# First microseconds of an mLSTM and two gated feed-forward layers: Exp table, forget factors, Sigmoids and first weights reordered

## The chip, the cores and the metric

One core of a Trainium2 chip runs the whole kernel in one launch. The metric is the device time of a run in microseconds; the time before is the median of three runs. The profile is of one execution on the chip.

## The reference, cut to what matters

```python
# q, k, v, o_gate: (B=4, H=8, S=768, D=40); i_gate, f_gate: (4, 8, 768)
for t in range(S):
    m_new = maximum(f_gate[t] + m, i_gate[t])
    f_stab = exp(f_gate[t] + m - m_new)
    i_stab = exp(i_gate[t] - m_new)
    m = m_new
    C = f_stab * C + i_stab * outer(v[t], k[t])
    n = f_stab * n + i_stab * k[t]
    y[t] = sigmoid(o_gate[t]) * (C @ q[t]) / maximum(abs(n @ q[t]), 1)
x = y as (3072 tokens, 320)
x = (sigmoid(x @ w_gate) * (x @ w_val)) @ w_out          # d_ff 1536
h = x @ w_in                                             # d_ff 2048
out = (h * clip(h + 3, 0, 6) / 6) @ w2_out
```

## The kernel before

The sequence is cut into 6 chunks of 128 steps. Within a chunk the recurrence is written as products of matrices: scores k by q, multiplied by a decay matrix, times v scaled by the input factor; between chunks a state is carried. All arithmetic is fp32; the dense layers split each operand into two parts and multiply three times.

**The start.** Lines 264 to 265 load the gates, 32 rows (batch and head) by 768 steps. `stabilise` (L207 to L219) runs a running maximum over some of the steps on VectorE and then two Exps on ScalarE, which give the forget factors `fz` and the input factors `i`. It is called for the first 128 steps first, and for the other 640 after batches 0 and 1 of chunk 0 are traced (L564). The forget factors of chunk 0 are stored to DRAM (L552), and `dec_load` (L192) reads them back per batch, broadcast to all 128 partitions, into the tile `dec`, 512 KB each. In `att0` a scan on VectorE (L320, two per batch) turns these rows into the decay matrix with the identity `ident4` as its second operand; L333 multiplies the scores (L303) by it. `transpose_rows` (L225) brings the input factors into columns (`iT`). The Sigmoid of the output gates (L338) is issued on ScalarE behind the first `stabilise`'s last Exp (`first_exp`); Exp and Sigmoid lie in different tables of ScalarE.

**After that**, `att1` (L340 on) forms numerator and denominator, and `att2` (L423 on) transposes the result into the token-column tiles `xh` and `xl` (L432, L433) that the first layer reads. Batches 0 and 1 of chunk 0 come first, then `later_chunks` (transposes of the other chunks' factors, the scan L239, the end values L252 and their copy L259), then the steps of the first layer: `m1_h` (matmuls L444 to L451) and `m1_out` (L486, L496). For chunk 0 the first four steps are done for batches 0 and 1, then for batches 2 and 3 (`halves`, L569), whose attention is traced among the steps.

**The weights** come as 64-bit words. `fetch` (L85) loads one tile of 640 KB into one of three buffers, `to_f32` unpacks it (L105 on ScalarE, L108, L112 and L116 on VectorE), and `split_in` or `split_out1` splits it (L134 to L154). The first three are fetched with batch 1's load (L558, L559).

**The order of the work.** Each engine runs its own queue in order. The order in a queue is written by a scheduler that follows the order of the program among what it expects to be ready, so it need not be the program's. All loads but the input gates' go through SP's queue (L189, L190, L193, L552, L88); the input gates' load is issued from ScalarE's queue. PSUM has eight banks: three `mm`, three `acc`, two `att`. In the start `any_ps` hands them out in turn, by a count; the later attention pieces take `att` banks.

Of the kernel before, what the change touches and what calls it, by code (L numbers as in the profile page):

```python
# [8 lines left out]
F32 = mybir.dt.float32  # L9
# [4 lines left out]
AF = mybir.ActivationFunctionType  # L14
# [4 lines left out]
B, H, S, D = 4, 8, 768, 40  # L19
L = 128  # L20
NC = S // L
BH = B * H
NP = H // 2
D1 = D + 1
P = 128
# [7 lines left out]
def mlstm_then_two_gated_ffn(  # L33
# [11 lines left out]
    nc = tc.nc  # L45

    const = ctx.enter_context(tc.tile_pool(name="const", bufs=1))
# [8 lines left out]
    def ps_mm():  # L56
        return mm_ps.tile([P, 512], F32, tag="mm", name="mm")

    def ps_acc():
        return acc_ps.tile([P, 512], F32, tag="acc", name="acc")  # L60

    def ps_att():
        return att_ps.tile([P, 512], F32, tag="att", name="att")
# [3 lines left out]
    def any_ps():  # L67
        k = banks_used[0] % 8
        banks_used[0] += 1
        return ps_mm() if k < 3 else ps_acc() if k < 6 else ps_att()  # L70

    ident4 = const.tile([P, 4, P], F32, name="ident4")
    ident = ident4[:, 0, :]
    half = const.tile([P, 1], F32, name="half")
    iT = const.tile([P, NC, B, H, 1], F32, name="iT")
    gT = const.tile([P, NC, B, H, 1], F32, name="gT")
    gend = const.tile([P, NC, B, NP, 1], F32, name="gend")
# [7 lines left out]
    def fetch(src):  # L85
        r = gpool.tile([P, 640], I64, tag="raw", name="raw", bufs=3)
        if src.shape == r.shape and src.dtype == I64:
            nc.sync.dma_start(out=r, in_=src)  # L88
            return r
        x = r.bitcast(F32)[:, 0:640]  # L90
        nc.sync.dma_start(out=x, in_=src)
        return x
# [76 lines left out]
    at = {}  # L169
# [5 lines left out]
    def slot_f32(n, p=P):  # L175

        return wpool.tile([P, 1280], F32, tag="w", name="early", bufs=18)[:p, :n]

    def att_load(c, b):
        if c == 0 and b > 1:  # L180
            t = slot_f32(2 * NP * L).rearrange("p (a n l) -> p a n l", a=2, l=L)
            v = slot_f32(3 * DM).rearrange("p (a n) -> p a n", a=3)
            d = slot_f32(H * L).rearrange("p (h l) -> p h l", l=L)
        else:
            t = ap.tile([P, 2, NP, L], F32, tag="qk", name="qk")
            v = ap.tile([P, 3, DM], F32, tag="vko", name="vko")
            d = ap.tile([P, H, L], F32, tag="dec", name="dec")
        at[c, b] = {"qk": t, "vko": v, "dec": d}
        nc.sync.dma_start(out=t, in_=qkT[c, b])  # L189
        nc.sync.dma_start(out=v, in_=vko[c, b])  # L190

    def dec_load(c, b):  # L192
        nc.sync.dma_start(  # L193
            out=at[c, b]["dec"].rearrange("p h l -> p (h l)"),
            in_=fz_dram[c, b * H : (b + 1) * H, :]
            .rearrange("h l -> (h l)")
            .rearrange("(o n) -> o n", o=1)
            .to_broadcast([P, H * L]),
        )

    f_sb, i_sb, m_sb, fz_sb, fs_sb, g_sb = [slot_f32(S + 1, BH) for _ in range(6)]
    fz = fz_sb[:, :S].rearrange("p (c l) -> p c l", l=L)
# [4 lines left out]
    def stabilise(a, b):  # L207

        m_old, m_new = m_sb[:, a:b], m_sb[:, a + 1 : b + 1]
        f, i = f_sb[:, a:b], i_sb[:, a:b]  # L210
        nc.vector.tensor_tensor_scan(
            out=m_new, data0=f, data1=i,
            initial=-1e30 if a == 0 else m_sb[:, a : a + 1], op0=ALU.add, op1=ALU.max,
        )
        nc.vector.tensor_tensor(out=f, in0=f, in1=m_old, op=ALU.add)
        nc.vector.tensor_tensor(out=f, in0=f, in1=m_new, op=ALU.subtract)
        nc.scalar.activation(out=fz_sb[:, a:b], in_=f, func=AF.Exp)
        nc.vector.tensor_tensor(out=i, in0=i, in1=m_new, op=ALU.subtract)
        return nc.scalar.activation(out=i, in_=i, func=AF.Exp).ins  # L219

    def transpose_rows(src, dst, chunks):

        ps = any_ps()
        for k, c in enumerate(chunks):
            nc.tensor.transpose(  # L225
                out=ps[:, k * BH : (k + 1) * BH], in_=src[:, c, :], identity=ident[:BH, :BH]
            )
        n = len(chunks)
        nc.scalar.copy(
            out=dst[:, chunks[0] : chunks[0] + n].rearrange("p c b h o -> p (c b h o)"),  # L230
            in_=ps[:, : n * BH],
        )

    def later_chunks():
# [26 lines left out]
            in_=ps[:, BH // 2 : NC * BH // 2],  # L261
        )

    nc.sync.dma_start(out=f_sb[:, :S], in_=gates[:, 0])
    nc.scalar.dma_start(out=i_sb[:, :S], in_=gates[:, 1])
    make_identity(nc, ident)
# [1 line left out]
    nc.vector.tensor_copy(out=ident4[:, 1:, :], in_=ident4[:, 0:1, :].to_broadcast([P, 3, P]))  # L268
    nc.gpsimd.memset(fs_sb[:, :S], 0.0)
    nc.gpsimd.memset(cst, 0.0)  # L270
    nc.vector.memset(half, 0.5)

    sel = const.tile([BH, BH // 2], F32, name="sel")
    nc.vector.tensor_reduce(
        out=sel, in_=ident[:BH, :BH].rearrange("p (n two) -> p n two", two=2),
# [4 lines left out]
        out=odd[:, :, 0], in_=ident[:BH, :BH].rearrange("p (n two) -> p two n", two=2),  # L280
# [4 lines left out]
        out=par.rearrange("p (two n) -> p two n", two=2), in_=odd.to_broadcast([BH, 2, 64])  # L285
    )

    def scale_heads(out, in_, by, apart):

        if apart:  # L290
            for h in range(H):
                nc.scalar.mul(out=out[:, h, :], in_=in_[:, h, :], mul=by[:, h, :])
        else:
            nc.vector.tensor_tensor(out=out, in0=in_, in1=by.to_broadcast(list(out.shape)), op=ALU.mult)


    def att0(c, b, ps):
        a = at[c, b]
        qk, dec = a["qk"], a["dec"]
        s_ps = [ps(), ps()]  # L300
        for h in range(H):
            p0 = 64 * (h % 2)
            nc.tensor.matmul(  # L303
                out=s_ps[h % 2][:, (h // 2) * L : (h // 2 + 1) * L],
                lhsT=qk[p0 : p0 + D, 1, h // 2, :],
                rhs=qk[p0 : p0 + D, 0, h // 2, :],
                start=h < 2,
                stop=h >= H - 2,
                skip_group_check=True,
            )  # L310
        vko_t = a["vko"]
        vi = ap.tile([P, H, D1], F32, tag="vi", name="vi")
        v_h = vko_t[:, 0, :].rearrange("p (h d) -> p h d", d=D)
        if c == 1:
            scale_heads(vi[:, :, 0:D], v_h, iT[:, c, b], True)
        nc.scalar.copy(out=vi[:, :, D:D1], in_=iT[:, c, b])

        for n in range(2):
            x = dec[:, 4 * n : 4 * n + 4, :].rearrange("p h l -> p (h l)")
            nc.vector.tensor_tensor_scan(  # L320
                out=x, data0=x, data1=ident4.rearrange("p h l -> p (h l)"),
                initial=0.0, op0=ALU.mult, op1=ALU.add,
            )
        if c != 1:
            scale_heads(vi[:, :, 0:D], v_h, iT[:, c, b], False)
        a["vi"] = vi
        if c < NC - 1:
            vd = ap.tile([P, H, D1], F32, tag="vd", name="vd")
            scale_heads(vd, vi, dec[:, :, L - 1 : L], c == 0 and b > 0)
            a["vd"] = vd  # L330
        for n in range(2):
            x = dec.rearrange("p (n two) l -> p two n l", two=2)[:, n]
            nc.vector.tensor_tensor(  # L333
                out=x, in0=s_ps[n].rearrange("p (n l) -> p n l", l=L), in1=x, op=ALU.mult
            )

        with tc.issue_after(first_exp):
            nc.scalar.activation(out=vko_t[:, 2, :], in_=vko_t[:, 2, :], func=AF.Sigmoid)  # L338

    def att1(c, b, ps):  # L340
# [182 lines left out]
    jobs = []  # L523
# [22 lines left out]
    fetched = []  # L546


    x_tiles((1, 0))
    att_load(0, 0)  # L550
    first_exp = stabilise(0, L)
    nc.sync.dma_start(out=fz_dram[0], in_=fz[:, 0, :])  # L552
    dec_load(0, 0)
    transpose_rows(i_c, iT, range(0, 1))
    for b in range(1, B):
        att_load(0, b)
        dec_load(0, b)
        if b == 1:  # L558
            fetched += [fetch(jobs[-1 - n][0]) for n in range(3)]  # L559
    for b in range(2):  # L560
        work(1 + b, n_w1)
        for att in (att0, att1, att2):
            att(0, b, any_ps)
    stabilise(L, S)  # L564
    later_chunks()


# [21 lines left out]
    for i, (c, f, ts) in enumerate(steps):  # L589
        if i == halves[0] - 1:  # L590
            for b in range(2):
                att_load(1, b)
                dec_load(1, b)
        for _ in range(quota[i]):
            if pieces:
                cp, b, piece = pieces.pop(0)
                if cp > 0 and b == 0 and piece == 0:
                    x_tiles((1, cp))
                (att0, att1, att2)[piece](cp, b, ps_att)
                nxt = divmod(cp * B + b + 2, B)  # L600
                if cp > 0 and piece == 2 and nxt[0] < NC:
                    att_load(*nxt)
                    dec_load(*nxt)
# [143 lines left out]
```

## Time and profile before

| | us |
|---|---|
| median of three runs | 881.5 |
| lowest and highest | 878.61, 883.31 |
| the profiled execution | 880.11 |
| its span | 878.3 |

The profiled execution's time is 1.8 us more than its span, which is what the profile shows from the first to the last instruction. PE is TensorE's matmuls, PEld its weight loads, DVE VectorE, ACT ScalarE, SP the engine whose queue issues most DMAs; SPq and ACTq are the queues themselves. The granted clock of TensorE was 0.998 in the mean. Times in the rows are microseconds from the start of the span.

### The profile page before, as it was taken

What the parts mean: (1) busy time and instruction counts of PE and PEld (TensorE: products, weight loads), DVE (VectorE), ACT (ScalarE), POOL (GpSimd) and SP (SyncE); (2) the same over time, 40 slices, a digit from 0 to 9 for tenths busy, and PEclk for the clock granted to TensorE, in tenths of its full rate; (3) what the DMA queues carried; (4) which work ended last, traced back from release to release, by engine and by line L of the source; (5) the groups of instructions that cost most, each with busy time, mean ns of one, the idle gap of its engine ahead of it and who ended that gap; (6) DMA issues with size and microseconds to landing.
All of it is one profiled execution on the core that took longest, in us unless ns stands there. A gap on an engine that the chain in (4) does not pass through costs nothing.

```text
span 878.3 us, 17029 instructions
## 1 busy us (share of the span) xinstructions
PE 839.8 (96%) x7173; PEld 720.3 (82%) x7173; DVE 537.9 (61%) x961; ACT 358.7 (41%) x716; POOL 2.5 (0%) x8
## 2 busy tenths in 40 slices
PE   2599999999999999999999999999999999999998
PEld 2488778887778888888788888999999999999997
DVE  7999996775787787776645555344343343443433
ACT  5876553222332233233225445334343343433433
POOL 1000000000000000000000000000000000000000
PEclk9999999999999999999999999999999999999999
DMA  9735544232444444455302321001010010000000
GB/s 322 276 119 182 168 162 140 91 120 94 144 133 153 162 160 153 162 165 196 104 1 84 92 92 72 1 1 66 1 66 1 1 67 1 31 0 1 31 1 31
DMA packets 25212, 84.49 MB, mean 96 GB/s; under 512 B 2608, under 2 KB 5872, under 8 KB 25136
## 3 DMA queue, kind: packets, MB, share of 16 engines
q1 hardware_dynamic: 25088, 83.31, 27.8%
q8 instruction: 56, 0.92, 0.4%
q14 instruction: 20, 0.16, 0.1%
q10 hardware_dynamic: 48, 0.10, 0.0%
HBM read 69.40 MB, written 13.99 MB: 95 GB/s over the span
## 4 chain that ended last, share of the span: by engine, by line
PE 85%; DVE 8%; DMA 4%; issue 2%; ACT 2%; SPq 0%; ACTq 0%; DVEq 0%
PE mm L448 11%; PE mm L450 11%; PE mm L449 11%; PE acc L486 10%; PE mm L444 6%; PE mm L451 6%; PE acc L653 5%; PE acc L652 5%; PE acc L651 5%; PE acc L496 3%; DMA dec<-fz_dram 3%; PE att L303 3%; DVE dec L320 2%; PE att L653 2%; PE att L651 2%; PE att L652 2%
## 5 line engine op out<-in xcount | busy, mean ns | idle before, releaser
L448 PE MATMUL mm<-xh,w 128*128 128x512 f32 (+1 forms) x520 | 195.1, 375 | 0.0
L450 PE MATMUL mm<-xh,w 128*128 128x512 f32 (+1 forms) x520 | 194.7, 374 | 0.0
L449 PE MATMUL mm<-xl,w 128*128 128x512 f32 (+1 forms) x520 | 194.4, 374 | 0.0
L457 ACT CAST gh<-g 128x512 fp32r<-128x512 f32 (+1 forms) x178 | 106.1, 596 | 199.5 <-DVE g L471 108.1
L458 DVE TENSOR_TENSOR gl<-g,gh 128x512 fp32r<-128x512 f32 (+1 forms) x178 | 117.4, 660 | 103.2 <-ACT gh L457 102.8
L633 DVE SCALAR_TENSOR_TENSOR g<-g,mm 128x512 f32<-128x512 f32 x96 | 66.0, 687 | 112.1 <-ACT g L632 112.0
L450 PEld LDWEIGHTS mm<-xh,w 128*128 128x128 f32 x520 | 97.8, 188 | 18.6
L449 PEld LDWEIGHTS mm<-xl,w 128*128 128x128 f32 x520 | 97.9, 188 | 18.4
L632 ACT ACTIVATE g<-mm,half 128x512 f32<-128x512 f32 x96 | 66.2, 690 | 112.1 <-PE mm L451 112.0
L448 PEld LDWEIGHTS mm<-xh,w 128*128 128x128 f32 x520 | 98.1, 189 | 14.1
L486 PE MATMUL acc<-gh,w 128*128 128x512 f32 (+1 forms) x328 | 105.4, 366 | 1.0 <-ACT gh L457 1.0
L444 PE MATMUL mm<-xl,w 128*128 128x512 f32 (+1 forms) x260 | 103.9, 400 | 1.0 <-DVE g L471 0.9
L451 PE MATMUL mm<-xh,w 128*128 128x512 f32 (+1 forms) x260 | 97.0, 373 | 0.0
L653 PE MATMUL acc<-w,gl 128*128 128x320 f32 x288 | 89.0, 309 | 0.0
L652 PE MATMUL acc<-w,gh 128*128 128x320 f32 x288 | 88.9, 309 | 0.0
L651 PE MATMUL acc<-w,gh 128*128 128x320 f32 x288 | 88.8, 308 | 0.0
L471 DVE TENSOR_TENSOR g<-g,mm 128x512 f32<-128x512 f32 (+1 forms) x82 | 50.7, 618 | 52.6 <-PE mm L451 52.0
L470 ACT ACTIVATE g<-mm 128x512 f32<-128x512 f32 (+1 forms) x82 | 44.7, 545 | 91.1 <-PE mm L451 90.8
L486 PEld LDWEIGHTS acc<-gh,w 128*128 128x128 f32 x328 | 60.7, 189 | 11.6 <-ACT gh L457 1.6
L486 PE MATMUL acc<-gl,w 128*128 128x512 f32 (+1 forms) x164 | 60.5, 370 | 3.0 <-DVE gl L458 3.0
L320 DVE TENSOR_TENSOR_SCAN dec<-dec,ident 128x512 f32<-128x512 f32 x44 | 52.5, 1214 | 15.0 <-DMA dec<-fz_dram 14.9
L444 PEld LDWEIGHTS mm<-xl,w 128*128 128x128 f32 x260 | 48.9, 188 | 12.2 <-issue 1.7
(142 smaller groups left out, 1096.9 us busy)
## 6 DMA issues: line engine op xcount, KB each, us to landing
raw<-in_w SPq DMA_DIRECT2D x20, 640.0 KB, 4.2
qk<-in_qkT SPq DMA_DIRECT2D x22, 512.0 KB, 4.1
dec<-fz_dram SPq DMA_DIRECT2D x22, 512.0 KB, 5.7
vko<-in_vko SPq DMA_DIRECT2D x22, 480.0 KB, 4.2
raw<-in_wo SPq DMA_DIRECT2D x14, 640.0 KB, 4.1
w_dram<-bits SPq DMA_DIRECT2D x16, 320.0 KB, 3.8
raw<-w_dram SPq DMA_DIRECT2D x16, 320.0 KB, 2.9
x_dram<-x SPq DMA_DIRECT2D x6, 768.0 KB, 5.7
```

Source lines behind the costliest of these rows:

```text
L320: nc.vector.tensor_tensor_scan(out=x, data0=x, data1=ident4.rearrange("p h l -> p (h l)"), initial=0.0, op0=ALU.mult, op1=ALU.add,)
L444: nc.tensor.matmul(out=banks[j], lhsT=tail, rhs=xl[:, 2, :], start=True, stop=False)
L448: nc.tensor.matmul(out=banks[j], lhsT=hi, rhs=xh[:, k, :], start=False, stop=False)
L449: nc.tensor.matmul(out=banks[j], lhsT=hi, rhs=xl[:, k, :], start=False, stop=False)
L450: nc.tensor.matmul(out=banks[j], lhsT=lo, rhs=xh[:, k, :], start=False, stop=False)
L451: nc.tensor.matmul(out=banks[j], lhsT=tail, rhs=xh[:, 2, :], start=False, stop=True)
L457: nc.scalar.copy(out=gh, in_=g)
L458: nc.vector.tensor_tensor(out=gl, in0=g, in1=gh.bitcast(F32), op=ALU.subtract)
L486: nc.tensor.matmul(out=a[m], lhsT=lhsT, rhs=rhs, start=st and lhsT is hi and rhs is gh, stop=en and lhsT is lo, skip_group_check=True,)
L651: nc.tensor.matmul(out=a, lhsT=gh[:, ts], rhs=hi, start=st, stop=False)
L652: nc.tensor.matmul(out=a, lhsT=gh[:, ts], rhs=lo, start=False, stop=False)
L653: nc.tensor.matmul(out=a, lhsT=gl[:, ts], rhs=hi, start=False, stop=en)
```

## The change

A dummy Exp on one column (`den0`) is traced ahead of everything else, with the memset of `half` that feeds it; it stands ahead of the input gates' DMA on ScalarE. For batch 0 the forget factors are no longer read back from DRAM: `dec_spread` multiplies one column of the identity, repeated 128 times, with the 32 rows of factors, for each of the eight heads, so that each row lies on all 128 partitions in two PSUM banks; the scan reads its first operand there. The store to DRAM stays, as batches 1 to 3 still read it. The first weight tile is fetched ahead of batch 1's q, k, v and gates; the next two after batch 1's factors. `stabilise` for the other 640 steps is traced ahead of the first attention, and the Sigmoids are issued behind both of its Exps.

```diff
+    den0 = const.tile([P, 1], F32, name="den0")
...
+    def dec_spread(b):
+
+        banks = [any_ps(), any_ps()]
+        for h in range(H):
+            r = b * H + h
+            nc.tensor.matmul(
+                out=banks[h // 4][:, (h % 4) * L : (h % 4 + 1) * L],
+                lhsT=ident[:BH, r : r + 1].to_broadcast([BH, P]),
+                rhs=fz[:, 0, :],
+                start=h % 4 == 0,
+                stop=h % 4 == 3,
+                skip_group_check=True,
+            )
+        at[0, b]["factors"] = banks
...
-        nc.scalar.activation(out=fz_sb[:, a:b], in_=f, func=AF.Exp)
+        exp = nc.scalar.activation(out=fz_sb[:, a:b], in_=f, func=AF.Exp).ins
         nc.vector.tensor_tensor(out=i, in0=i, in1=m_new, op=ALU.subtract)
-        return nc.scalar.activation(out=i, in_=i, func=AF.Exp).ins
+        return exp, nc.scalar.activation(out=i, in_=i, func=AF.Exp).ins
...
+    nc.vector.memset(half, 0.5)
+
+    nc.scalar.activation(out=den0, in_=half, func=AF.Exp)
     nc.sync.dma_start(out=f_sb[:, :S], in_=gates[:, 0])
     nc.scalar.dma_start(out=i_sb[:, :S], in_=gates[:, 1])
...
-    nc.vector.memset(half, 0.5)
...
-                out=x, data0=x, data1=ident4.rearrange("p h l -> p (h l)"),
+                out=x, data0=a["factors"][n] if "factors" in a else x, data1=ident4.rearrange("p h l -> p (h l)"),
...
-        with tc.issue_after(first_exp):
+        with tc.issue_after(exps[0]), tc.issue_after(exps[1]):
             nc.scalar.activation(out=vko_t[:, 2, :], in_=vko_t[:, 2, :], func=AF.Sigmoid)
...
     att_load(0, 0)
-    first_exp = stabilise(0, L)
+    fetched.append(fetch(jobs[-1][0]))
+    att_load(0, 1)
+    stabilise(0, L)
     nc.sync.dma_start(out=fz_dram[0], in_=fz[:, 0, :])
-    dec_load(0, 0)
+    dec_spread(0)
     transpose_rows(i_c, iT, range(0, 1))
-    for b in range(1, B):
+    dec_load(0, 1)
+    fetched += [fetch(jobs[-1 - n][0]) for n in range(1, 3)]
+    for b in range(2, B):
         att_load(0, b)
         dec_load(0, b)
-        if b == 1:
-            fetched += [fetch(jobs[-1 - n][0]) for n in range(3)]
+    exps = stabilise(L, S)
     for b in range(2):
         work(1 + b, n_w1)
         for att in (att0, att1, att2):
             att(0, b, any_ps)
-    stabilise(L, S)
     later_chunks()
```

## Rows read from the trace of the kernel before

**Rows 1.** The page's busy times: us, share of the span, instructions.
```profile
PE 839.8 (96%) x7173; PEld 720.3 (82%) x7173; DVE 537.9 (61%) x961; ACT 358.7 (41%) x716; POOL 2.5 (0%) x8
```

**Rows 2.** Busy times by stage: stretch, length, each engine's busy us, clock, DMA share, GB/s.
```profile
0.00:13.27 13.27, 4.37 (x33) 4.08 (x33) 6.86 (x19) 8.20 (x13) 2.49 (x8) 1.00 0.84 267
13.27:43.28 30.01, 13.34 (x325) 10.35 (x324) 28.54 (x52) 21.78 (x71) 0.00 (x0) 1.00 0.81 314
43.28:80.00 36.72, 34.20 (x461) 30.74 (x460) 34.82 (x77) 25.20 (x77) 0.00 (x0) 1.00 0.47 151
...
200.00:800.00 600.00, 600.00 (x4537) 510.82 (x4534) 337.22 (x566) 225.43 (x389) 0.00 (x0) 1.00 0.24 80
```

**Rows 3.** The chain that ended last, in order of time: start, us, what.
```profile
5.53 0.33 SPq L552
...
6.37 6.06 DMA raw<-in_w
```

**Rows 4.** The timeline of VectorE: start, us, instruction, idle time before it and its releaser.
```profile
9.33 0.21 DVE L284 COPY par<-odd 32x128 f32<-32x128 f32 x1
...
10.19 0.16 DVE L236 COPY early<-early 32x5 f32<-32x5 f32 x1 [0.65 <-ACT early L217]
...
10.96 0.49 DVE L294 TENSOR_TENSOR vi<-vko,iT 128x320 f32<-128x320 f32 x1 [0.20 <-DMA vko<-in_vko]
...
13.27 0.49 DVE L108 TENSOR_SCALAR bits<-u 128x640 int32<-128x640 int32 x1 [1.81 <-ACT u L105]
...
32.44 0.56 DVE L433 TENSOR_TENSOR xl<-acc,xh 128x384 fp32r<-128x384 f32 x1 [1.05 <-ACT xh L432]
```

**Rows 5.** The timeline of ScalarE (first and last of six table loads) and SP's queue.
```profile
3.70 1.28 ACT L219 ACT_TABLE_LOAD   x1 [3.70 <-DMA early<-in_gates]
...
5.00 0.31 ACT L219 ACTIVATE early<-early 32x128 f32<-32x128 f32 x1
...
9.11 0.80 SPq L193 DMA_DIRECT2D dec<-fz_dram  x2
...
23.76 1.28 ACT L338 ACT_TABLE_LOAD   x1
```

**Rows 6.** Busy times from the start to three moments; the last number is GB/s.
```profile
0.00:7.90 7.90, 0.00 (x0) 0.00 (x0) 4.18 (x10) 3.34 (x5) 2.49 (x8) 1.00 0.73 230
0.00:10.70 10.70, 1.80 (x11) 1.51 (x13) 6.30 (x16) 6.09 (x9) 2.49 (x8) 1.00 0.81 263
0.00:18.40 18.40, 4.75 (x33) 4.17 (x33) 11.96 (x24) 10.37 (x15) 2.49 (x8) 1.00 0.89 303
```

**Rows 7.** The timeline of PE: eight score matmuls, two records each.
```profile
9.87 2.08 PE L303 MATMUL mm<-qk 40*128 40x128 f32 x16
```

**Rows 8.** VectorE's instructions to 130 us by line and shape: busy us, mean ns.
```profile
L320 DVE TENSOR_TENSOR_SCAN dec<-dec,ident 128x512 f32<-128x512 f32 x12 | 14.5, 1216 | 0.0
...
L137 DVE TENSOR_TENSOR w<-bits,w 128x512 fp32r<-128x512 f32 x12 | 8.2, 681 | 0.6 <-ACT w L134 0.5
...
L333 DVE TENSOR_TENSOR dec<-att,dec 128x512 f32<-128x512 f32 x8 | 5.5, 683 | 0.5 <-PE att L303 0.5
```

**Rows 9.** The timeline: batch 2's second score product, the end values' copy, the second half.
```profile
39.22 0.67 DVE L333 TENSOR_TENSOR early<-att,early 128x512 f32<-128x512 f32 x1
...
40.16 0.23 ACT L259 COPY gend<-acc 128x80 f32<-128x80 f32 x1 [0.86 <-PE acc L252]
...
63.39 0.39 PE L444 MATMUL mm<-xl,w 128*128 128x256 f32 x1
```

**Rows 10.** Busy times (columns as in rows 2) and PE's timeline around 113 us.
```profile
111.00:113.00 2.00, 0.75 (x2) 0.66 (x3) 1.97 (x4) 1.51 (x4) 0.00 (x0) 0.76 0.73 210
113.00:115.00 2.00, 2.00 (x6) 1.07 (x4) 2.00 (x5) 0.56 (x2) 0.00 (x0) 0.50 0.88 354
...
113.27 0.63 PE L486 MATMUL acc<-gl,w 128*128 128x512 f32 x1
...
119.64 0.39 PE L486 MATMUL acc<-gh,w 128*128 128x512 f32 x1
```

## The prediction

> **What bounds the kernel now.** I read four views, in this order. The busy times of the page say that PE is busy for 96% of the span [rows 1], so what can be saved is PE's idle time, 38.5 us in all. The busy times by stage say where that idle time lies: PE does 17.7 us of work in the first 43.3 us, has 2.5 us of idle time from 43.3 to 80 us, and none from 200 to 800 us [rows 2]. The stage to look at is therefore the first 43.3 us, up to the first step of the first feed-forward layer (L444). In its second part, from 13.27 us on, VectorE is busy 28.5 of 30.0 us, while ScalarE has 8 us and PE 17 us to spare [rows 2]: VectorE sets the pace there, and it still does up to 80 us (34.8 of 36.7). So the start of VectorE's unbroken run of work decides when PE fills up. The chain in order of time tells what that run waits for: the first weights are issued at 6.37 us, behind the store of the forget factors that had to wait for Exp, and land at 12.43 [rows 3]; ScalarE unpacks them in 0.8 us, and VectorE starts at 13.27 [rows 4]. VectorE's own rows show what this costs. It is done with the setup work at 9.54 (9.33 + 0.21), and then sits idle for 0.65, 0.20 and 1.81 us, 2.66 us in all [rows 4].
>
> **The parts of the change.**
>
> Exp's table. The profile has six table loads of 1.28 us before 26 us; Exp starts 1.30 us after its load does [rows 5]. Afterwards two should be left, since the Sigmoids now queue behind both long Exps: four loads or 5.1 us less on ScalarE. I count nothing for them, because ScalarE has 8 us of slack in the stage [rows 2]. If that cover were gone, they would be worth at most their 5.1 us. The early load also lets the two short Exps start as soon as VectorE has their input instead of at 5.00 [rows 5]. I estimate 0.3 us from the gap, which nothing uses, as VectorE has other work up to 9.54. One cost is unknown: the dummy Exp stands ahead of ScalarE's DMA for the input gates. If the DMA is issued behind it, the gates come later by the load and an Exp, 1.28 + 0.31 = 1.6 us; if ahead of it, by nothing. I take nothing, because the DMA waits for no one and the dummy waits for a memset on VectorE; 1.6 us goes to the range. A Sigmoid held back costs nothing: its result is first read by the output product, long after.
>
> The factors of batch 0. Eight fp32 matmuls replace a 512 KB load that went through DRAM. Eight of 40x128 took 2.08 us [rows 7], so I take 2.1 us for the new ones; they run from about 5.2 us, when PE is idle (it has no instruction up to 7.9 us [rows 6]). The factors are then in PSUM at 7.3 us, before VectorE is free. Before, the store was issued at 5.53 and the loads at 9.11 [rows 3, 5], so that no scan stands among VectorE's rows up to 13.27. Now two scans (1.22 us each [rows 8]) can fill the time from 9.54 to 12.0 that was idle. The scans read one operand from PSUM. VectorE's 128x512 pass took 683 ns with an operand in PSUM and 681 ns without [rows 8], so I count nothing. [...] Two PSUM banks more are taken, which moves every later user of the eight banks by two places; its price is a rival below.
>
> The first weights. They move from behind the store to the fourth place of SP's queue. Bytes up to them are gates 0.20, q and k 0.52, v, k and o 0.49, weights 0.66 MB: 1.87 MB. The rows give 230 GB/s up to 7.9 us, or 1.82 MB, and 263 GB/s up to 10.7, or 2.81 MB [rows 6]. In the kernel before, 2.88 MB were queued up to the weights and had moved by about 10.9 us; the weights landed at 12.43, 1.5 us later. The 1.87 MB have moved by 8.1, so the weights should land at 8.1 + 1.5 = 9.6 instead of 12.43, and unpacking (0.8 us on ScalarE) lets VectorE go on with them at 10.4. What is moved back is q, k and v, k, o of batch 1, by 0.66 MB or some 2 us, to 11 and 12.5 us. Their readers, the score matmuls and the scaling of v of batch 1, find the scans and weights of batch 0 ahead of them. On SP the two other weight loads still wait behind the loads that wait for the store.
>
> The long gate recursion. Traced earlier, it gets no new work, and VectorE already did it before 9.54. Only its second Exp is freed from the table switch. POOL's queue loses and gains nothing.
>
> **The sum.** VectorE has work at hand from 9.54 (scans 2.4 us, then the weights at 10.4), so the 2.66 us of idle time go; no other engine adds to the path. From 13.27 to 43.28 I leave its idle 1.47 us where they are: 1.05 of them end with a ScalarE cast of batch 0's output [rows 4], which the change doesn't touch. The first step then starts at 40.6 instead of 43.28, and as nothing in the change touches PE's later work or waits, the end moves as much. The profiled execution took 880.1 us for a span of 878.3; 880.1 - 2.7 = 877.4. It lies 1.4 us under the median of 881.5, so against the median this is 878.8 us, 0.3% less. A measurement of this kernel tells some 0.5%, or 4.4 us, from no change.
>
> **The rivals.**
>
> Faster by more. The idle time left in VectorE's stage goes too: 2.66 + 1.47 = 4.1 us before the first step, and 1.9 us between 43.3 and 80 us [rows 2], 6.0 us in all, or 875.5 against the median. It needs ScalarE's freed 5.1 us to pull in the chain of batch 0's output. For it speaks that the longest later wait, 1.05 us, is one for ScalarE [rows 4]. Against it: that is one wait, and ScalarE was not full. [...] Chance 0.27.
>
> No gain. The load of batch 1's factors takes the place of the wait removed. It still goes through DRAM, and SP may issue the next weights and batch 2 ahead of it: then 5.7 MB are ahead of or in it, and by 18.4 us 5.6 MB had moved [rows 6], so it would land at about 20 us (18.8 and the 1.5 us of above). VectorE's order is fixed, so a scan put early stands in front of everything behind it and eats the 2.7 us: 881.5. Against it: there is work of two weight tiles to put ahead. Chance 0.18.
>
> Slower. The two factor banks shift the banks, and the scores of batch 2 get the two that the transposed decay and its end values hold until the copy at 40.16 to 40.39 [rows 9]. The scores then run from 40.4 to 42.5 (2.08 us [rows 7]) and their products (0.68 each [rows 8]) to 43.9, where before the second product ended at 39.89 [rows 9]: 4.0 us late. Batch 3 follows in the same two banks, and the second half of the first tile, at 63.39 [rows 9], needs it: 885.5 against the median. [...] Against it: the copy waits for VectorE alone, which starts sooner, and a bank that an earlier reader has left can serve instead. Chance 0.10.
>
> **How the numbers follow.** My forecast has 0.45. Faster by over 0.5%: the first rival, 0.27. Slower by over 0.5%: the third, 0.10. Within: forecast and second, 0.63. The range goes from 874.5, where the first rival gives 1 us more, to 883.5, which takes in the late gates and a part of the third.
>
> **What would show it.** Two table loads before 30 us instead of six; the weights landed before 10.5 us; VectorE without a gap over 0.3 us from 9.5 to 14; the first L444 at 40 to 41.5 us. A first L444 at 43 or later, or PE idle time over 3 us between the first step and 80 us, would make it wrong.

## The result, and the profile after

The changed kernel takes 888.1 us in the median of five runs (887.28 to 890.07) against 881.5 us before: 1.0085 times as long, with a 95% interval of 1.006 to 1.011. The forecast was 878.8 us, 0.3% less than before, with a range up to 883.5. The profiled execution after took 890.07 us for a span of 888.3 us, the longest of its five; the one before lay 1.4 us under its median. So the two traces differ by 10.0 us where the medians differ by 6.6.

The page's busy times and PE's granted clock in 40 slices, after:

```profile
PE 855.7 (96%) x7189; PEld 734.0 (83%) x7189; DVE 538.1 (61%) x961; ACT 354.8 (40%) x713; POOL 2.5 (0%) x8
...
PEclk9997999999999999999999999999999999999999
```

PE's idle time fell, from 38.5 us (878.3 - 839.8 [rows 1]) to 32.6 us. But its busy time rose by 15.9 us, for the same output plus 16 small matmul records. The fourth slice of the clock, about 67 to 89 us, shows a 7.

Busy times by stage, columns as in [rows 2]:

```profile
0.00:13.27 13.27, 6.99 (x38) 6.53 (x39) 7.26 (x19) 6.62 (x13) 2.49 (x8) 1.00 0.76 268
13.27:44.03 30.76, 17.80 (x272) 13.37 (x270) 27.38 (x51) 19.62 (x68) 0.00 (x0) 1.00 0.77 292
44.03:80.00 35.97, 34.05 (x463) 30.06 (x463) 28.57 (x59) 18.52 (x56) 0.00 (x0) 0.91 0.32 111
80.00:151.29 71.29, 67.48 (x594) 55.67 (x593) 65.83 (x132) 40.42 (x102) 0.00 (x0) 0.95 0.46 156
200.00:800.00 600.00, 599.77 (x4646) 509.36 (x4645) 339.74 (x575) 223.73 (x387) 0.00 (x0) 1.00 0.24 82
```

From 200 us on nothing has changed. The granted clock that the view gives is 0.91 and 0.95 in the stages up to 151 us, where it was 1.00 up to 80 us before [rows 2] (its 1.00 at the start is not what PE had, see below), and VectorE, at work for 34.8 of 36.7 us there before, has 7 us idle.

SP's queue and ScalarE's timeline at the start, after:

```profile
2.11 0.43 SPq L89 DMA_DIRECT2D raw<-in_w  x1
...
12.47 0.33 SPq L209 DMA_DIRECT2D dec<-fz_dram  x1
```
```profile
8.81 0.73 ACT L233 ACTIVATE early<-early 32x640 f32<-32x640 f32 x1
9.56 1.28 ACT L356 ACT_TABLE_LOAD   x1
10.85 0.47 ACT L356 ACTIVATE vko<-vko 128x320 f32<-128x320 f32 x1
11.23 0.76 ACT L106 ACTIVATE u<-raw 128x640 f32<-128x640 f32 x1
```

The weights are issued at 2.11 us (6.37 before [rows 3]) and land 7.6 us later, at 9.7. But ScalarE unpacks them only at 11.23: it takes the Sigmoids' table and batch 0's Sigmoid first. There are two table loads in all, as planned (the other is at 1.18). Batch 1's factors are asked for at 12.47, since their store to DRAM took 7.0 us to land.

VectorE's timeline, after:

```profile
9.64 0.16 DVE L252 COPY early<-early 32x5 f32<-32x5 f32 x1 [0.87 <-ACT early L233]
...
12.02 0.49 DVE L109 TENSOR_SCALAR bits<-u 128x640 int32<-128x640 int32 x1 [1.20 <-ACT u L106]
...
13.97 0.82 DVE L117 SCALAR_TENSOR_TENSOR bits<-u,bits 128x640 int32<-128x640 int32 x1
14.70 2.33 DVE L338 TENSOR_TENSOR_SCAN dec<-mm,ident 128x512 f32<-128x512 f32 x2
...
26.87 0.67 DVE L351 TENSOR_TENSOR dec<-mm,dec 128x512 f32<-128x512 f32 x1
...
28.46 0.68 DVE L351 TENSOR_TENSOR dec<-mm,dec 128x512 f32<-128x512 f32 x1
```

The 2.66 us of waits [rows 4] have become 0.87 and 1.20. The unpacking starts 1.25 us sooner than before (12.02 for 13.27), not 2.9. The scans of batch 0 stand behind it in the queue, so their factors, ready in PSUM at 11.5, are read at 14.70 to 17.0. Batch 1's score products come at 26.87 and 28.46; before, they came at 21.74 and 23.07. VectorE's first of them before, and PE's scores of batch 2 before:

```profile
21.74 0.68 DVE L333 TENSOR_TENSOR dec<-att,dec 128x512 f32<-128x512 f32 x1
...
28.12 2.08 PE L303 MATMUL att<-early 40*128 40x128 f32 x16
```

PE's timeline, after:

```profile
5.73 2.08 PE L321 MATMUL acc<-qk 40*128 40x128 f32 x16 [5.73 <-DMA qk<-in_qkT]
7.74 3.77 PE L198 MATMUL mm<-early,ident 32*128 32x128 f32 x16
...
12.11 2.07 PE L321 MATMUL mm<-qk 40*128 40x128 f32 x8 [0.54 <-ACT iT L245]
15.97 2.07 PE L321 MATMUL mm<-qk 40*128 40x128 f32 x8 [1.79 <-DVE dec L338]
...
39.19 0.68 PE L268 MATMUL att<-ge,par 32*128 32x80 f32 x2 [0.77 <-DVE ge L264]
39.80 1.22 PE L321 MATMUL att<-early 40*128 40x128 f32 x6
...
42.45 1.64 PE L321 MATMUL att<-early 40*128 40x128 f32 x10
44.03 0.58 PE L462 MATMUL mm<-xl,w 128*128 128x256 f32 x1
...
50.05 0.41 PE L467 MATMUL mm<-xl,w 128*128 128x256 f32 x1
50.27 0.33 PE L468 MATMUL mm<-xh,w 128*128 128x256 f32 x1
50.44 0.28 PE L466 MATMUL mm<-xh,w 128*128 128x256 f32 x1
...
73.62 0.41 PE L466 MATMUL mm<-xh,w 128*128 128x256 f32 x1
```

The spread takes 3.77 us, behind batch 0's scores. The second half of batch 1's scores waits until the first factor bank is read (15.97). Batch 2's scores, at 28.12 before, are at 39.80, right behind the end values: the two `att` banks of the rival "Slower", at its place. The first step is at 44.03 instead of 43.28.

The last four rows are matmuls of one shape, 128x256. At 73.62, where the granted clock is 0.50, one takes 0.41 us; from 50.44 on, at 1.00, one takes 0.28. Up to 50.05 they take 0.41 too, although the windows print 1.00 there. So PE ran its first steps at the lower level, up to about 50.4 us. Before, the full level came right behind the first step, at about 43.8 us:

```profile
43.66 0.33 PE L448 MATMUL mm<-xh,w 128*128 128x256 f32 x1
43.83 0.28 PE L449 MATMUL mm<-xl,w 128*128 128x256 f32 x1
```

**Where the 10 us lie.** I follow PE from its first step to the first copy of the finished first tile's swapped half (ScalarE, `sw` from `acc`), which came at 142.26 before and 151.29 after; the rest, 736.0 and 737.0 us, is nearly the same. In 50 equal windows of that stretch, busy time times (1 - granted clock) is what the clock takes away by the windows. The half-speed start, which the windows miss, is half of the time from the first step to the moment at which the 128x256 matmuls go from 0.41 to 0.28 us (43.76 before, 50.37 after, 45.78 in e3, 48.05 in e9, 47.77 in e14, 45.42 in e15; in e2 and e5 the windows have it, in e11 there is none). It is an estimate: it takes all of that time as worth half. The rest of the busy time is work at full speed. The same sums for some experiments, told below, stand with them:

| profiled execution | first step | tile done | between | PE idle | clock, by the windows | half-speed start | work |
|---|---|---|---|---|---|---|---|
| before | 43.28 | 142.26 | 98.98 | 5.90 | 1.47 | 0.24 | 91.37 |
| after | 44.03 | 151.29 | 107.26 | 5.73 | 6.77 | 3.17 | 91.59 |
| e2, bank count moved alone | 43.76 | 149.66 | 105.90 | 4.18 | 10.82 | 0 | 90.90 |
| e3, no spread | 42.92 | 148.08 | 105.16 | 5.81 | 6.69 | 1.43 | 91.23 |
| e5, e2 and end values in `acc` | 43.06 | 146.62 | 103.56 | 4.75 | 7.28 | 0 | 91.53 |
| e9, after, waits filled | 43.93 | 148.97 | 105.04 | 6.02 | 3.40 | 2.06 | 93.56 |
| e11, before, waits filled | 42.82 | 141.27 | 98.45 | 5.58 | 0.02 | 0 | 92.85 |
| e14, after, unpack first | 37.77 | 149.54 | 111.77 | 5.91 | 8.18 | 5.00 | 92.68 |
| e15, no spread, unpack first | 43.14 | 144.04 | 100.90 | 5.80 | 1.66 | 1.14 | 92.30 |

After minus before is 0.75 at the first step, 5.30 for the clock by the windows, 2.93 for the half-speed start, 0.22 of work and -0.17 of idle time: 9.03 us, of which 8.23 are the clock. These are sums over one execution of each; no run moves the clock alone. The falls by the windows come behind PE's waits. Two-microsecond windows of after (columns as in [rows 2]):

```profile
64.00:66.00 2.00, 1.50 (x9) 1.09 (x10) 1.92 (x5) 0.60 (x2) 0.00 (x0) 1.00 0.79 251
66.00:68.00 2.00, 1.67 (x12) 1.25 (x10) 1.78 (x5) 1.75 (x4) 0.00 (x0) 0.86 0.19 77
68.00:70.00 2.00, 2.00 (x7) 1.55 (x8) 1.75 (x4) 0.00 (x0) 0.00 (x0) 0.50 0.03 8
...
82.00:84.00 2.00, 0.51 (x4) 0.54 (x5) 1.87 (x6) 1.80 (x9) 0.00 (x0) 1.00 0.27 113
84.00:86.00 2.00, 2.00 (x13) 1.55 (x12) 2.00 (x5) 1.35 (x4) 0.00 (x0) 0.63 0.22 44
```

By the windows the granted 0.50 lasted from about 67.4 to 74.3 and from 84.5 to 91.3; before there was one stretch, half as long, at 113 [rows 10].

### The profile page after: what moved, and what is told of

Same layout as the page of the kernel before. It is cut to its first block, busy times and chain, and to the rows that moved or that the text cites. A ratio compares the mean times of both kernels' runs of the same rounds, so it can differ in the third digit from the quotient of the medians.

```text
span 888.3 us, 17059 instructions
## 1 busy us (share of the span) xinstructions
PE 855.7 (96%) x7189; PEld 734.0 (83%) x7189; DVE 538.1 (61%) x961; ACT 354.8 (40%) x713; POOL 2.5 (0%) x8
## 4 chain that ended last, share of the span: by engine, by line
PE 85%; DVE 9%; DMA 4%; ACT 1%; issue 1%; DVEq 0%; SPq 0%
PE mm L466 11%; PE mm L468 11%; PE mm L467 11%; PE acc L504 10%; PE mm L462 6%; PE mm L469 6%; PE acc L673 5%; PE acc L672 5%; PE acc L671 5%; PE acc L514 3%; PE att L321 3%; DMA dec<-fz_dram 3%; DVE dec L338 2%; PE att L673 2%; PE att L672 2%; PE att L671 2%
## 5 line engine op out<-in xcount | busy, mean ns | idle before, releaser
L468 PEld LDWEIGHTS mm<-xh,w 128*128 128x128 f32 x520 | 99.6, 192 | 18.6
L467 PEld LDWEIGHTS mm<-xl,w 128*128 128x128 f32 x520 | 99.7, 192 | 18.4
L466 PEld LDWEIGHTS mm<-xh,w 128*128 128x128 f32 x520 | 99.8, 192 | 14.2
L462 PEld LDWEIGHTS mm<-xl,w 128*128 128x128 f32 x260 | 49.7, 191 | 12.0 <-issue 3.2
L338 DVE TENSOR_TENSOR_SCAN dec<-dec,ident 128x512 f32<-128x512 f32 x42 | 50.1, 1215 | 14.7 <-DMA dec<-fz_dram 14.7
```

What stands on the lines that cost most here:

```text
L338: nc.vector.tensor_tensor_scan(out=x, data0=a["factors"][n] if "factors" in a else x, data1=ident4.rearrange("p h l -> p (h l)"), initial= ...
L462: nc.tensor.matmul(out=banks[j], lhsT=tail, rhs=xl[:, 2, :], start=True, stop=False)
L466: nc.tensor.matmul(out=banks[j], lhsT=hi, rhs=xh[:, k, :], start=False, stop=False)
L467: nc.tensor.matmul(out=banks[j], lhsT=hi, rhs=xl[:, k, :], start=False, stop=False)
L468: nc.tensor.matmul(out=banks[j], lhsT=lo, rhs=xh[:, k, :], start=False, stop=False)
```

## The experiments

All ratios are to the kernel before, run on the same chip, with 95% intervals.

### The banks of batch 2

e1 puts the factors into the two `att` banks, so that the count of `any_ps` does not move. e2 is the kernel before with the count moved alone.

```diff
-        banks = [any_ps(), any_ps()]     # e1, in the changed kernel
+        banks = [ps_att(), ps_att()]
-    banks_used = [0]                     # e2, in the kernel before
+    banks_used = [2]
```

> The changed kernel, but the spread factors take the two att banks directly, so that the count by which the start hands out its banks is where it was before the change. Theory A (the count moved by two: batch 2's scores wait for the two att banks that the transposed decay and the end values take, the second half of the first tile comes late, PE's gaps bring the granted clock down): batch 2's scores (L321 att<-early) start before 33 us instead of at 39.80, the xl tile of batch 3 is written by 60 us instead of 66.16, no stretch at half clock between 60 and 92 us, 876 to 880 us. Theory B (the loss is made before the first step, by the new order of weights, Sigmoids and SP's queue): first step still at about 44 us and 886 to 889 us.

> The kernel before, with nothing changed but that the count of banks starts at 2 instead of 0. Theory A: batch 2's scores start at about 39 us instead of 28.12, the xl tile of batch 3 is written at 64 to 67 us instead of 60.03, TensorE's clock falls to half between 60 and 95 us, 885 to 889 us. Theory B: 880 to 883 us, as before, since no work is moved.

e1: 887.13 us, 1.0058 (1.0037 to 1.0079). e2: 887.05 us, 1.0056 (1.0034 to 1.0078). PE's timeline of e2:

```profile
38.63 0.68 PE L252 MATMUL att<-ge,par 32*128 32x80 f32 x2 [0.77 <-DVE ge L248]
39.24 1.18 PE L303 MATMUL att<-early 40*128 40x128 f32 x4
```

So moving the count by two makes the order of the rival "Slower", and costs over half a per cent without any other part of the change. But e1, whose scores of batch 2 are at 29.6 us, is as slow, and its first step is later still, at 45.56: there batch 1's scores wait for the factors' banks until 15.4.

e5 is e2, and e6 the changed kernel, with the later chunks' transposes and end values in the `acc` banks, so that nothing holds batch 2's two.

```diff
-        ps = any_ps()                                          # transposes
+        ps = any_ps() if len(chunks) == 1 else ps_acc()
-        ps = any_ps()                                          # end values
+        ps = ps_acc()
```

> The kernel before with the count of banks starting at 2, as in the run that was 0.56% slower, but the transposes and end values of the later chunks take acc banks, so that the two att banks are free for batch 2. If those two banks are what the moved count costs (theory A): batch 2's scores before 33 us instead of 39.24, batch 3's xl tile by 61 us instead of 64.33, 879 to 883 us, the same as before. If the moved count costs through other users of the banks, or through the order of everything (theory C): batch 2's scores early, but still 885 to 888 us.

> The changed kernel, complete, with the transposes and end values of the later chunks in acc banks. Theory A: batch 2's scores at about 29 to 33 us instead of 39.80, batch 3's xl tile by 61 us instead of 66.16, 879 to 883 us. Theory C: 885 to 889 us; batch 1's scores still wait for the banks of the factors.

e5: 887.65 us, 1.0067 (1.0042 to 1.0092). e6: 888.72 us, 1.0081 (1.0058 to 1.0104). Batch 2's scores were back at 30.28 and 27.4 us, and the time stayed. The theory that these two banks set the time falls here: they were late, but not the cause.

e7 puts the factors of the changed kernel into `acc` banks; e8 is the kernel before with the spread alone, in `acc` banks.

```diff
-        banks = [any_ps(), any_ps()]
+        banks = [ps_acc(), ps_acc()]
```

> The changed kernel with the spread factors in two acc banks, count not moved: batch 1's scores then have the att banks to themselves and need not wait for batch 0's scans (they waited until 15.42 us with the factors in the att banks), and batch 2's scores come before the later chunks. Theory A with that second wait: first step at 40 to 42 us, batch 3's xl tile by 60 us, 874 to 880 us, the best of all. Theory C: 883 to 888 us, as the scan's order is made anew in any case.

> The kernel before with the spread alone, factors in two acc banks, count not moved. Theory A: better than the spread with the moved count (885.9), first step at 40 to 42 us, 876 to 881 us. Theory C: 883 to 887 us.

e7: 887.88 us, 1.0054 (1.0037 to 1.0072). e8: 886.13 us, 1.0053 (1.0033 to 1.0073). With the count as before and other banks, the spread still costs half a per cent. In e8 VectorE does batch 2's score products (32.8 and 35.5 us) ahead of batch 1's output, and the first step is at 44.96.

### The parts

e3 takes the spread out of the changed kernel; e4 is the kernel before with the spread as its only change.

```diff
-    dec_spread(0)          # e3; the reverse in e4
+    dec_load(0, 0)
```

> The changed kernel, but batch 0's factors are read back from DRAM as before, so that the two banks are not taken; table, Sigmoids and first weights as changed. Theory A: the count is not moved, 877 to 882 us. Theory B: 885 to 889 us, as the new order of weights and Sigmoids is still there.

> The kernel before with the spread of batch 0's factors alone (banks from the same count). Theory A: the count moves, so 885 to 889 us although a transfer of 512 KB goes. Theory B: 879 to 882 us, as weights and Sigmoids are where they were.

e3: 883.41 us, 1.0013 (0.9991 to 1.0035). e4: 885.93 us, 1.0046 (1.0025 to 1.0067). With the spread, in this order of the work, the change is slower; table, Sigmoids and first weights together are worth nothing that can be measured, in place of 0.3%.

### What a fall of the clock costs

e13 puts eight waits into PE's steady work in the second layer, where PE never waited and the order of the work around it stays: a chain of copies on VectorE that begins at a bank of the step before and ends in the weights of the next (they get the bank times zero added, so they keep their values).

```diff
+        if (c, n) in stalls:
+            stall(slots["in2", n][:, :, 256:384], last_banks[0][1], stalls[c, n])
         h_pair(slots["in2", n], (2, c), banks)
```

> The kernel before with eight waits put into PE's steady work of the second layer, where it never waits and its granted clock is 1.00: ahead of steps (0,2), (0,6), (1,2), (1,6), (2,2), (2,6), (3,2), (3,6) a chain of 6, 8, 10, 12, 14, 16, 20 and 24 copies of 128x512 on VectorE that begins at the step before and ends in the weights of this one. Theory clock: waits of PE up to about 1 us cost their own length; behind one of some 2 us or more the granted clock stands at 0.50 for several us, so that the wait costs 3 to 5 us more than its length. Rival, clock falls only because little work is queued in that part of the kernel: each wait costs its own length, and the granted clock stays at 1.00 or falls in the wait alone.

One run, 921.78 us, 38.2 us over the median of before beside it (883.59). PE's waits, four of the eight, and the windows behind the second of these four:

```profile
547.45 0.51 PE L444 MATMUL mm<-xl,w 128*128 128x512 f32 x1 [0.87 <-DVE w L634]
...
640.53 0.50 PE L444 MATMUL mm<-xl,w 128*128 128x512 f32 x1 [2.02 <-DVE w L634]
...
675.64 0.50 PE L444 MATMUL mm<-xl,w 128*128 128x512 f32 x1 [4.56 <-DVE w L634]
...
747.85 0.80 PE L444 MATMUL mm<-xl,w 128*128 128x512 f32 x1 [7.33 <-DVE w L634]
```
```profile
638.00:640.00 2.00, 0.51 (x4) 0.24 (x2) 1.86 (x5) 0.00 (x0) 0.00 (x0) 1.00 0.00 0
640.00:642.00 2.00, 1.47 (x6) 1.24 (x7) 0.44 (x2) 0.00 (x0) 0.00 (x0) 0.99 0.03 8
642.00:644.00 2.00, 2.00 (x6) 1.57 (x5) 0.12 (x1) 0.69 (x1) 0.00 (x0) 0.50 0.00 0
644.00:646.00 2.00, 2.00 (x7) 1.57 (x7) 1.26 (x2) 0.62 (x1) 0.00 (x0) 0.65 0.00 0
```

The waits of 0.17 and 0.87 us cost their length. Each of the four from 2.02 to 4.56 us was followed by one stretch at 0.50, which took 1.70 to 1.72 us of full-speed time (here 0.02 + 1.00 + 0.70); in three of the four it begins only when PE is at work again. Behind the waits of 7.3 and 7.6 us the loss is 3.42 us, half of it in the wait itself. The eight waits are 29.1 us, six times 1.70 while PE worked makes 10.2: 39.3 us, about what was measured. The rival, that only the busy start of the kernel makes the clock fall, is out. The table's losses by the windows lie near one such price in before and e15, two in e9 and four in e3 and after, where they are two stretches of twice the length; those of e2, e5 and e14 lie at no multiple.

### Filling the waits

If waits bring the falls, matmuls nobody reads should prevent them. e9 adds to the changed kernel 9 matmuls of 128x256 ahead of batch 3's transposes and 14 ahead of the scores of chunk 1's batch 1; e10 does so to e3 and e11, with 9 and 8, to the kernel before. e12 is e5 with 9 and 8, and 7 more of 128x128 ahead of batch 0's transposes.

```diff
+    def keep_busy(bank, n):
+        x = XH[1, 0][:, 0, 0 : T // 2]
+        for _ in range(n):
+            nc.tensor.matmul(out=bank[:, 0 : T // 2], lhsT=x[:, 0:P], rhs=x, start=True, stop=True, skip_group_check=True)
...
+        if (c, b) == (0, 3):
+            keep_busy(x_ps, 9)
```

> The changed kernel with 23 more matmuls of 128x256 whose results nobody reads: 9 in the bank of batch 3's transposes, 14 in the bank of batch 5's scores, both of which stand in PE's order right where PE waited (61.27 and 64.50 us). They add about 2.5 us of PE work at 0.11 us each. Theory clock: the waits of PE between 60 and 67 us are what the granted clock falls behind, and the fall costs more than the waits; with them filled the stretch at 0.50 from 66 to 75 is gone, the clock loss between 40 and 200 us goes from 6.8 to about 3 us, and the kernel takes 884 to 886 us although PE does more. Rival, VectorE's chain sets the time and the clock is low only while PE would wait anyway: the extra matmuls bring nothing back, 888 to 891 us.

> The changed kernel with the factor load in place of the spread (883.4 us before this edit), and the same 23 idle matmuls. Theory clock: the stretch at 0.50 from 62 to 70 us, which cost some 3.2 us, goes, 880 to 881.5 us, which is faster than the kernel before. Rival, VectorE's chain: 883.5 to 886 us.

> The kernel before with 17 of the idle matmuls at the same two places, a control. It has no fall of the clock between 40 and 110 us to save, so by the theory of the clock they can only cost their own 1.8 us or less: 881.5 to 883.5 us. By the rival that any shift in the order of the work costs half a per cent, 885 to 887 us, since the planner's order of VectorE's work shifts too.

> The kernel before with the bank count moved by two, the later chunks' end values in the bank pair of the accumulators (887.65 us before this edit), with 7 idle float32 transposes' worth ahead of batch 0's transposes (PE waits from 27.6 to 29.4 us there, and the clock is at 0.50 from 28 to 48 us), and 17 idle matmuls as above. Theory clock: its clock loss of 9.2 us goes down to 3 to 5 us, and it takes 880 to 883 us. Rival, VectorE's chain: 887 to 890 us.

e9: 888.82 us, 1.0080 (1.0055 to 1.0106). e10: 883.13 us, 1.0004 (0.9985 to 1.0022). e11: 880.14 us, 0.9971 (0.9954 to 0.9988). e12: 883.09 us, 1.0009 (0.9994 to 1.0024). In the profiles the losses by the windows fell, in e9 to 3.40 and in e11 to 0.02. But the changed kernel gained nothing in its median. What the added matmuls cost is not shown: e9's profile is 2.6 us shorter than after's, but it is the fastest execution of e9's five, and after's is the slowest of its five. e12 gained half a per cent on e5, and the kernel before 0.3%, where the clock theory had expected a small loss; e10 and e11 fell outside both of their ranges. In e11's profile the clock still stood at 0.50, from 29 to 42.8 us, but that ended as the first step began; its mean granted clock, 0.992, is lower than the 0.998 of before, and its time is shorter. So in this kernel a low clock ahead of the first step, where PE mostly waits, costs little, and the mean over the span does not tell what the clock costs.

e16 and e17 fill e14 and e15 (below) with 9 and 8; e18 leaves only the 9 in e11.

> The changed kernel with the unpack ahead of the Sigmoid (883.4 us), and 17 of the idle matmuls at the two places of the control. Theory clock, with the price that the measured waits gave (1.70 us of full-speed work for one fall): one or two of the falls at 64 to 72 and 116 to 127 us go, the matmuls cost up to 1.8 us, 880 to 882.5 us. Rival, the order in which the planner puts VectorE's work decides, and the matmuls shift it: anywhere from 880 to 888 us, with the number of falls following the order and not the filled waits.

> The changed kernel without the spread, with the unpack first (882.7 us), and the same 17 idle matmuls. Theory clock: only the fall at 112 to 118 us is left in its profile, far from the filled places, so the matmuls cost up to their 1.8 us and return nothing there: 882 to 884.5 us. Rival, order decides: 880 to 888 us.

> The kernel before with only the 9 idle matmuls ahead of batch 3's transposes, of the 17 that made it 0.29% faster. Theory clock: the fall at 112 us of the kernel before was avoided through the filled wait, so half of the matmuls keep at most half of the gain, 879.5 to 883 us. Rival, the gain came from the shifted order of VectorE's work (batch 1's scan of the next tile sooner), which the 9 alone cause too: 879 to 881 us.

e16: 883.62 us, 1.0013 (0.9999 to 1.0028). e17: 883.58 us, 1.0011 (0.9995 to 1.0027). e18: 882.72 us, 1.0000 (0.9982 to 1.0018). None is a gain. In e16's profile the fall at 64 us is gone and a new one stands at 76 to 87; e17 has one at 64 to 71, a place that was filled. So filled waits do not settle how many falls there are: the matmuls also shift the order of VectorE's work. e11 remains the only version faster than both kernels, by 0.3%; it was not repeated, and e18, with half of its matmuls, shows nothing.

### The unpack behind the Sigmoid

e14 is the changed kernel, and e15 that without the spread, with batch 0's Sigmoid queued behind the first unpack.

```diff
-        nc.scalar.activation(out=u, in_=upper.bitcast(F32), func=AF.Copy, scale=2.0**-112)
+        us.append(nc.scalar.activation(out=u, in_=upper.bitcast(F32), func=AF.Copy, scale=2.0**-112).ins)
...
-        with tc.issue_after(exps[0]), tc.issue_after(exps[1]):
+        with tc.issue_after(exps[0]), tc.issue_after(exps[1]), tc.issue_after(us[0]):
```

> The changed kernel with batch 0's Sigmoid queued behind the first unpack of the weights on ScalarE (11.23 us before this edit). Both theories: the unpack at 9.7, the three bit operations at 10.2 to 12.0, the scans of batch 0 at about 12.5 instead of 14.70. Theory order (what ScalarE does ahead of the unpack is what took the expected gain): the factor banks come free 2 us sooner, the first step is at 42 us or before, 882 to 885 us. Rival, the two banks of batch 2 and the clock set the time: the first step moves less than 0.5 us, 887 to 889 us.

> The changed kernel without the spread (883.4 us before this edit), with the same edit; PE's order does not change and VectorE's by three instructions. Theory order: the two idle stretches of VectorE ahead of 13 us go, all its work up to the first step comes some 1 to 2 us sooner, 880 to 882 us. Rival, the clock and the waits between 55 and 90 us set the time whatever is gained ahead of the first step: 882.5 to 884.5 us.

e14: 883.37 us, 0.9999 (0.9980 to 1.0017). e15: 882.73 us, 1.0006 (0.9988 to 1.0024). The intervals of e14 and of the changed kernel are far apart: one instruction's place, with the order that the scheduler then writes, brings back the whole loss. ScalarE's and VectorE's timelines of e14, and PE's first step and the first 128x256 matmul that took 0.28 us:

```profile
9.52 0.76 ACT L108 ACTIVATE u<-raw 128x640 f32<-128x640 f32 x1
10.30 1.28 ACT L358 ACT_TABLE_LOAD   x1
```
```profile
10.81 0.47 DVE L111 TENSOR_SCALAR bits<-u 128x640 int32<-128x640 int32 x1
...
13.73 2.33 DVE L340 TENSOR_TENSOR_SCAN dec<-mm,ident 128x512 f32<-128x512 f32 x2
...
22.20 0.69 DVE L353 TENSOR_TENSOR dec<-mm,dec 128x512 f32<-128x512 f32 x1
```
```profile
37.77 0.58 PE L464 MATMUL mm<-xl,w 128*128 128x256 f32 x1 [0.52 <-DVE xl L453]
...
47.88 0.28 PE L470 MATMUL mm<-xh,w 128*128 128x256 f32 x1
```

VectorE has no gap over 0.1 us from 9.71 to 23.9 us. Its scans come only 1.0 us sooner than after's, but batch 1's first score product comes at 22.20 instead of 26.87, and the first step at 37.77: 5.5 us sooner than before. And still the kernel is no faster than before. The table says why for the profiled execution (887.02 us, the slowest of ten): PE ran at the lower level up to 47.8 us, 10 us from the first step on, which takes 5.0 of the 5.5 us back, and the falls by the windows take 6.7 us more than before; work at full speed grew by 1.3 us, and idle time did not. What sets the moment at which PE comes to the full level, no run isolates. e15 is the clean case: PE's order is that of e3 and VectorE's differs by the places of a few instructions of the first unpack, and the two are not told apart.

## Why the prediction was wrong

- **Loads, landing, tables: right.** The gates' DMA stayed ahead of the dummy's table load (issued at 0.73, so the 1.6 us of the range did not come), two table loads are left, and the weights landed at 9.7 (forecast 9.6). The rows after show 1.29 us from the load (9.56) to the Sigmoid (10.85), as [rows 5] showed 1.30 from the load to the Exp.
- **"VectorE has work at hand from 9.54 (scans 2.4 us, then the weights at 10.4)": the step that failed first.** The unpacking came at 12.02, the scans at 14.70, and the first step at 44.03 instead of 40.6, beyond the 43 us that the prediction had named as a sign of being wrong. It rested on two costs put at nothing. The table load and Sigmoid were covered by ScalarE's 8 us of slack, an average over the stage; at 9.56 to 11.23 they stood in front of the one unpack that VectorE waited for. And "a Sigmoid held back costs nothing" looked at its reader, not at what its table load would hold up. e14 shows what the order is worth: with the unpack first, and all that the scheduler then moves, 888.1 goes to 883.4 us.
- **The spread's 2.1 us: mis-sized, 3.77 measured.** The price was taken from score matmuls that alternate between two halves of the partitions, 130 ns a record; the spread's come from 32 partitions alone, 236 ns a record. They also began at 7.74 us instead of 5.2, as batch 0's scores stood ahead of them on PE. Its banks were then read at 14.70 to 17.0 and not at 9.54 to 12.0, so batch 1's scores waited 1.79 us. e3 and e4 show that the spread, with the order it brings, costs some half a per cent.
- **"The end moves as much": wrong even where the first step does move, and the larger part of the miss.** It took PE's speed behind the first step as given: the sum puts the clock at nothing, and "what can be saved is PE's idle time" counts time at half speed as work. In the profiles the clock took 8.23 us more than before, by the windows and the half-speed start, where idle time fell by 0.17. e14 has the first step 5.5 us sooner and is a tie. PE's idle time between the first step and the tile's end is 4.2 to 6.0 us in every row of the table.
- **"Slower" had the right place and a wrong cause.** Batch 2's scores did go behind the end values. But e5 and e6 freed those banks and stayed as slow. Its 885.5 counts nothing for the granted clock, and so lies 0.4 us short of the 0.5% that its chance is for. In the two profiles the clock is the larger part: where the windows print 0.50, a 128x512 matmul took 0.63 us instead of 0.39 [rows 10]; before had one such stretch, 1.47 us by the windows, after had two, of 3.4 us each, and 3.17 us of half-speed start.

What stays open: which single wait sets off each fall in the first 130 us, what sets the end of the half-speed start, and how the order of VectorE's work leads to either. Executions of one kernel differ in it: 79 of the kernel before, beside e1 to e15, had mean granted clocks from 0.985 to 1.00 and spans from 877.7 to 885.1 us, so a profiled execution's falls are one draw, and e3's and e14's profiles lie above their medians.

## What to carry to other kernels

Slack of an engine over a stage hides nothing at the moment when another engine waits for one of its instructions: look at what its queue holds between the data's arrival and the instruction that is waited for, table loads first. Where a scheduler writes the queues, taking two PSUM banks or delaying one operation re-orders the work far behind it, here for half a per cent with no work added; run the re-ordering alone, as e2, before crediting or blaming the edit. A step that starts sooner is worth only what PE's total idle time and its clock lose. Hold the lengths of matmuls of one shape beside the granted clock that a view prints: here the view gave 1.00 up to 50 us, where a 128x256 matmul took 0.41 us as at a granted 0.50, and not 0.28.

## What the runs showed of the hardware

- After's 128x256 matmuls took 0.41 us up to 50.05 us and 0.28 from 50.44 on; where the windows print a granted clock of 0.50 they took 0.41.
- In steady work a wait of PE of 0.87 us cost itself; one of 2.02 us was followed, 1.4 us after work had resumed, by a granted clock of 0.50 that took 1.7 us more. In the dense start of the first layer falls came behind shorter waits too: after's at 67.4 us follows waits of 0.50, 1.09 and 0.33 us.
- float32 score matmuls of 40x128 that alternate between two halves of the partitions took 130 ns a record (16 in 2.08 us), those of one half alone 259 ns (8 in 2.07 us), and the spread's, all from the same 32 partitions, 236 ns; all of these lie ahead of 50 us, where one score record of after lasted 417 ns from start to end in the median, against 272 from 81 to 144 us. The alternating scores also alternate between two PSUM banks; no run separates the two.
- A scan with its first operand in PSUM took 1208 ns, against 1217 ns from SBUF: that operand's place cost nothing, as the prediction had it.
- The 16 KB store of the factors took 7.0 us to land beside the loads of the start.
